# A spectral filter and a gated MLP on one core: the last eight first-stage columns become a fourth fold, and two rounds of w_out are lent to the lone transform pieces

## The chip, the cores and the metric

The kernel runs on one core of a Trainium2 chip. The metric is device time in microseconds of one execution, given as the median of several runs. The engines are TensorE (PE: matrix products, into the eight banks of PSUM), VectorE (DVE), ScalarE (ACT), GpSimd (POOL) and SyncE (SP, which issues transfers). Each takes its instructions in the order in which they were written out; between engines there are semaphores.

## The reference

```python
X = np.fft.rfft(x, axis=1)                 # x: 8 x 3008 x 256, fp32
y = np.fft.irfft(X * (filt_r + 1j*filt_i)[None], n=3008, axis=1)
h = y.reshape(24064, 256) @ w_in           # 256 x 2048
out = (h / (1 + np.exp(-h)) * h) @ w_out   # 2048 x 256
```

So each of 8 batches goes through a Fourier filter along its 3008 tokens, and every token then through a two-layer network with a gate between the layers.

## The kernel before

**The network.** The tokens of a batch form six pairs of blocks (256, 256 and 240 tokens to a block). For one pair the 2048 hidden channels are worked through in eight steps, so a batch has 48 steps and the whole 384. Both layers use a scheme with seven block products instead of eight. `hidden(step)` issues the seven products of w_in, `project(step)` the seven of w_out, one step behind (`LAG`). A step has eight rounds: in each, `hidden` and then `project` advance to their next `yield`, so that the products alternate. The products of w_in are called A11, A12, S2, S1, S3, A22, S4 in the order of their issue; A11, S2, S3 and A22 accumulate in one PSUM bank (`px`, tag x), A12, S1 and S4 in another (`pyz`, tag yz). After each of A11, S2 and S3, ScalarE copies the running sum away (`abc`) before the next product may add to it, and VectorE combines `pyz` with these copies into the operands `g` of the second layer. The products of w_out accumulate over the eight steps in four banks `acc` (tags a0 to a3). Two banks (tag f) are left for the transform.

**The transform.** The length 3008 is 32 x 94. For batches 2 to 7, first-stage products turn the 32 columns of x into residues (into DRAM tensor `d1`), a forward stage takes these (`load_t2`, `forward_two`), the filter is applied, an inverse stage writes `d2`, and a last stage (`load_wide`, `stage3_wide`, `turn_wide`, `copy_wide`, `fold_wide`) writes the network's input `y`. While the network works on one batch, the transform of the next is done in pieces between its steps. Batch b = 0 is done ahead of the steps, and b = 1 by a plan of its own.

**First stage.** Three folds (f = 0, 1, 2) take eight columns each. `load_fold` loads columns and their mirror images (`xr`, a copy of x with reversed rows) into `x_all`; `fold` has four parts on VectorE that form sums and differences; `stage1_fold` has sixteen products of 24 rows by 32 columns, 512 wide, in four banks; `evict_fold` copies two of these to SBUF and `pairs_fold` combines them with the other two and stores, on POOL's queue, to `d1`. The last eight columns go another way: `load_x` and `sums` for u = 6 and 7, `stage1` with four products of 47 rows by 64 columns each (L440, table `wf_t`), and `pairs_t1`.

**What sets the order.** `put(step, round, piece)` enters a piece in a list; `until` plays it out at its time. Steps below are counted within the 48 of the batch whose network is running. A piece is in one of three kinds of place. *Joined* pieces stand at the end of a step (round 7): the last-stage pieces k = 1, 2, 3 at steps 40, 0 and 8, with the folds f = 1 and 2 behind those at 40 and 0. In the next step (*opened*) the first two products of w_out are issued ahead of the first of w_in, and `project` is held in rounds 0 and 2. Pieces placed with `open_step` stand at the start of a step, after two products of w_out: the last eight columns at step 4 and the first last-stage piece, k = 0, at step 38. This last is also *early_out*: two more products of w_out follow the piece, and `project` is held in rounds 0, 2, 3 and 5:

```python
held = work[1:] if rnd in ((0, 2, 3, 5) if step in early_out else (0, 2) if step in opened else ()) else []
```

Which bank a piece uses is given by its `home`: the tags x and yz (`HIDDEN`), an `acc` bank's number, or None for tag f. A bank that the network also uses must be emptied before the next product of `hidden` or `project` can write it: bank a0 of a joined last-stage piece is emptied by VectorE (`turn_wide`), bank a1 by ScalarE (`copy_wide`).

Of the kernel before, what the change touches and what calls it, by code (L numbers as in the profile page):

```python
# [136 lines left out]
def dft_tables():  # L137

    wf = np.zeros((128, 2, 64))
    for par in range(2):  # L140
        for i, idx in enumerate(ORDER):
            ph = 2 * np.pi * (np.arange(N1) * (2 * idx + par) % 94) / 94
            for h in range(2):
                wf[64 * h:64 * h + N1, par, 2 * i] = np.cos(ph)
                wf[64 * h:64 * h + N1, par, 2 * i + 1] = -np.sin(ph)

# [59 lines left out]
    return (wf.astype(f32), wx.reshape(96, 128).astype(f32), wq.astype(f32), wi.astype(f32),  # L206
# [41 lines left out]
def kernel(  # L248
# [12 lines left out]
    wf_host, wx_host, wq_host, wi_host, d_host, e_host = dft_tables()  # L261
    wf_dram = nc.inline_tensor(wf_host, name="wf_tbl")
# [38 lines left out]
    wf_t = cpool.tile([128, 2, 64], FP32)  # L301
# [52 lines left out]
    def spectral(b):  # L354
# [42 lines left out]
        def load_x(u, queue=None):  # L397


            xs[u] = x_t[u % 2]  # L400
            if b == 1:
                xs[u] = xs[u].rearrange("p a n -> p (a n)")
                return load_rows(xs[u], u, 1, queue)
            for h in range(2):
                for r0, nr in ((0, 32), (32, N1 - 32)):
                    nc.sync.dma_start(
                        out=xs[u][64 * h + r0:64 * h + r0 + nr],
                        in_=bass.AP(tensor=x.tensor,
                                    offset=x.offset + (b * S + 32 * r0 + 4 * (u - 3) + 2 * h) * C,
                                    ap=[[32 * C, nr], [32 * N1 * C, 2], [1, 2 * C]]))  # L410
# [7 lines left out]
        def sums(u):  # L418
            ut = x_t[0] if u == 7 else upool.tile([128, 2, 512], FP32, name=f"u_{b}_{u}", tag="u")
            xt = xs.pop(u)  # L420
            for par, op in ((0, ALU.add), (1, ALU.subtract)):
                nc.vector.tensor_tensor(out=ut[0:111, par], in0=xt[0:111, 0], in1=xt[0:111, 1], op=op)
            us[u] = ut

        def stage1(u, ahead=True):
            t1 = tpool.tile([128, 2, 2, C], FP32, name=f"t1_{b}_{u}", tag="t")
            ps = [bank(b, f"pa_{b}_{u}_{h}", HIDDEN[h] if b > 1 and u == 6 else None) for h in range(2)]
            if b == 1:
                xt = xs.pop(u)
                for h in range(2):  # L430
                    nc.tensor.matmul(out=ps[h].rearrange("p n c -> p (n c)"), lhsT=wx_t,
                                     rhs=xt[0:96, 512 * h:512 * h + 512], start=True, stop=True)
                if ahead and u + 2 < 8:
                    load_x(u + 2)
            else:
                ut = us.pop(u)
                for par in range(2):
                    for h in range(2):
                        rows = slice(64 * h, 64 * h + N1)
                        nc.tensor.matmul(out=ps[h][64 * par:64 * par + 64], lhsT=wf_t[rows, par],  # L440
                                         rhs=ut[rows, par], start=True, stop=True)
            if b > 1 and u == 7:
                us["q1"] = t1, ps
                return
            for h in range(2):
                copy = nc.scalar.copy if b == 1 or h == 0 else nc.vector.tensor_copy
                copy(out=t1[:, h], in_=ps[h])  # L447
            if b == 1:
                us["t1", u] = t1
                if ahead:  # L450
                    store_rows(u)
                return
            us["p1"] = t1
# [12 lines left out]

        def pairs_t1(h):
            q, ps = us["q1"]
            p = us["p1"]
            butterfly(p[:, h], q[:, h], ps[1 - h])  # L470
            if h == 0:
                return
            for par in range(2):
                rows = slice(64 * par, 64 * par + 2 * NS)
                nc.gpsimd.dma_start(out=d1[par].rearrange("s p n c -> (s p) n c")[:, 12:16, :],
                                    in_=p[rows].rearrange("p h n c -> p (h n) c"))
                for ri in range(2):
                    nc.gpsimd.dma_start(
                        out=d1[par, :, 1 - ri, 28:32],
                        in_=q[64 * par + ri:64 * par + 2 * NS:2].rearrange("p h n c -> p (h n) c"))  # L480
# [41 lines left out]
        def stage1_fold(f):  # L522
            ut = us.pop("f")
            rhs = x_all[:, 0, 0], x_all[:, 1, 0], ut[:, 0], ut[:, 1]
            home = (*HIDDEN, *ACCS) if f == 0 else (*HIDDEN, 3, None)
            ps = [bank(b, f"pf_{b}_{f}_{q}", home[q]) for q in range(4)]
            for k in range(4):
                for q in range(4):
                    rows = slice(32 * q, 32 * q + 24)
                    nc.tensor.matmul(out=ps[q][32 * k:32 * k + 32], lhsT=wq_t[rows, k], rhs=rhs[k][rows],  # L530
                                     start=True, stop=True)
# [297 lines left out]
        return dict(us=us, store_rows=store_rows, evict_y=evict_y, pairs_t1=pairs_t1, halves=halves, load_first=load_first, stage1_first=stage1_first, fill_first=fill_first, load_x=load_x, load_two=load_two, sums=sums, stage1=stage1, reverse_x=reverse_x,  # L829
# [6 lines left out]
    joined, opened, early_out = set(), set(), set()  # L836
# [8 lines left out]
    def plan(b, part):  # L845
# [109 lines left out]
    def plan_rest(b, part):  # L955
# [6 lines left out]
        else:  # L962
# [7 lines left out]
            for k, step, places in ((1, -8, ((1, 5), (2, 5), (3, 3), (3, 5))), (2, 0, ((1, 5), (3, 5), (5, 3), (5, 5))),  # L970
# [8 lines left out]
                joined.add(at + step)  # L979
                opened.add(at + step + 1)  # L980
# [83 lines left out]
    def project(step):  # L1064
# [368 lines left out]
    for step, t, dram in ((20, wf_t, wf_dram), (20, wq_t, wq_dram), (40, dn_flat, dn_dram),  # L1433
                          (40, en_flat, en_dram), (30, wm_t, wm_dram)):
        put(step, 0, lambda t=t, dram=dram: nc.sync.dma_start(out=t, in_=dram.ap()))
# [19 lines left out]
    combines = ((-2, 1), (6, 1), (11, 5), (22, 5), (26, 6), (38, 1))  # L1455
# [15 lines left out]
    until(-1e-3)  # L1471
    for step in range(n_steps + LAG):
# [7 lines left out]
        if step in opened:  # L1480
# [41 lines left out]
```

## Time and profile before

| | |
|---|---|
| runs | 2527.57, 2528.6, 2530.13 us; median 2528.6 |
| profiled execution | 2527.65 us, of it the span 2525.8 us |
| granted clock of TensorE | 0.997 of full speed over the span |
| PEld, DVE, ACT, POOL busy | 85%, 69%, 43%, 17% of the span |
| transfers | 171.49 MB, mean 68 GB/s |

A group is a line of the kernel with an engine, an operation and its operands. A product of fp32 operands appears as two records. A record's length is the time from its start to its modelled end, longer than the time until the next can start; records that follow each other overlap. In the timeline several records of one group are one line: start, time from the first start to the last end, engine, line, operands, count, and in brackets the idle time of the engine before it with what ended that. Line numbers are those of the kernel before, unless it is said otherwise.

### The profile page before, as it was taken

To read this page: it belongs to the slowest core of one execution; us is meant where nothing else is said; L and a number is where in the kernel's file an instruction comes from. 1 tells how busy PE (TensorE), PEld (TensorE's weight loads), DVE (VectorE), ACT (ScalarE), POOL (GpSimd) and SP (SyncE) were. 2 spreads that over 40 slices of the span, in tenths; PEclk is the share of its full clock that TensorE was granted. 3 is DMA by queue.
4 is the path that set the end of the run, shared out by engine and by line. 5 is a ranking of instruction groups with operands and counts; after the bars stand their busy time and mean duration, and the time that the engine had idled before them with its cause. 6 is when DMAs were issued, how large, how long until landed. Compare 5 with 4: busy or idle time off the path is not lost. (4 is left out here: it accounts for less than half of the span.)

```text
span 2525.8 us, 42128 instructions
## 1 busy us (share of the span) xinstructions
PE 2504.1 (99%) x16122; PEld 2140.9 (85%) x16122; DVE 1750.5 (69%) x3621; ACT 1095.2 (43%) x3012; POOL 433.7 (17%) x679
## 2 busy tenths in 40 slices
PE   8999999999999999999999999999999999999999
PEld 6788888888888888888888888888888888888988
DVE  7866777777767777677777777767677766655544
ACT  3544444444444444444444444444444444444443
POOL 3211211022111121211221112211122111100100
PEclk9999999999999999999999999999999999999999
DMA  9522242212332132420324203331042211200000
GB/s 293 166 68 88 65 107 59 80 51 64 75 86 61 42 80 59 92 74 23 93 55 110 62 25 76 84 75 43 26 103 64 55 43 34 63 21 9 17 9 17
DMA packets 145218, 171.49 MB, mean 68 GB/s; under 512 B 21396, under 2 KB 118772, under 8 KB 144132
## 3 DMA queue, kind: packets, MB, share of 16 engines
q1 hardware_dynamic: 119752, 117.85, 18.0%
q0 software_dynamic: 22272, 45.68, 7.1%
q10 hardware_dynamic: 2992, 5.28, 0.7%
q8 instruction: 126, 2.06, 0.3%
q14 instruction: 76, 0.62, 0.1%
HBM read 96.88 MB, written 81.26 MB: 71 GB/s over the span
## 5 line engine op out<-in xcount | busy, mean ns | idle before, releaser
L1083 PE MATMUL acc<-g,w_t 128*128 128x256 f32 (+1 forms) x5376 | 1509.0, 376 | 4.2 <-DVE q L818 3.7
L1083 PEld LDWEIGHTS acc<-g,w_t 128*128 128x128 f32 x5376 | 1017.0, 190 | 150.4 <-DVE q L818 18.9
L989 DVE TENSOR_TENSOR g<-pyz,abc 128x256 f32<-128x256 f32 (+1 forms) x1152 | 479.1, 416 | 501.1 <-ACT abc L1039 259.8
L989 DVE TENSOR_TENSOR g<-g 128x256 f32<-128x256 f32 (+3 forms) x1152 | 589.6, 512 | 196.6 <-ACT g L1022 183.4
L1018 PE MATMUL px<-ty,w_t 128*128 128x256 f32 (+1 forms) x2304 | 679.2, 376 | 1.7 <-ACT abc L1033 0.7
L1022 ACT ACTIVATE g<-g 128x256 f32<-128x256 f32 (+1 forms) x1152 | 472.9, 410 | 243.1 <-DVE g L989 243.1
L989 POOL TENSOR_TENSOR s<-s 128x256 f32<-128x256 f32 (+1 forms) x329 | 251.7, 782 | 1467.0 <-DVE s L1101 1099.9
L1018 PEld LDWEIGHTS px<-ty,w_t 128*128 128x128 f32 x2304 | 432.8, 190 | 65.5 <-ACT abc L1033 7.0
L1018 PE MATMUL pyz<-y,w_t 128*128 128x256 f32 (+1 forms) x1536 | 452.7, 376 | 0.8 <-DVE g L989 0.6
L1018 PEld LDWEIGHTS pyz<-y,w_t 128*128 128x128 f32 x1536 | 283.2, 189 | 46.2 <-DVE g L989 6.9
L1033 ACT COPY abc<-px 128x256 f32<-128x256 f32 (+1 forms) x384 | 141.1, 368 | 368.1 <-PE px L1018 368.1
L1039 ACT COPY abc<-px 128x256 f32<-128x256 f32 (+1 forms) x384 | 141.5, 368 | 313.2 <-PE px L1018 313.1
L1022 ACT ACTIVATE g<-px 128x256 f32<-128x256 f32 (+1 forms) x384 | 145.8, 380 | 302.3 <-PE px L1018 302.3
L1018 PE MATMUL px<-y,w_t 128*128 128x256 f32 (+1 forms) x768 | 227.4, 378 | 1.5 <-DVE y L775 1.5
L1018 PE MATMUL pyz<-ty,w_t 128*128 128x256 f32 (+1 forms) x768 | 226.0, 376 | 0.2 <-DVE g L989 0.2
L1018 PEld LDWEIGHTS px<-y,w_t 128*128 128x128 f32 x768 | 143.9, 190 | 26.7 <-ACT t L447 4.9
L1018 PEld LDWEIGHTS pyz<-ty,w_t 128*128 128x128 f32 x768 | 142.2, 190 | 21.4 <-DVE g L989 1.0
L1026 ACT COPY abc<-px 128x256 f32<-128x256 f32 (+1 forms) x384 | 135.1, 352 | 37.3 <-PE px L1018 37.3
L1101 ACT COPY s<-acc 128x512 f32<-128x512 f32 (+1 forms) x94 | 54.2, 577 | 47.6 <-issue 28.6
L646 POOL DMA_DIRECT2D d<-low x36 | 22.2, 618 | 289.0 <-DVE low L642 289.0
L818 DVE STREAM_TRANSPOSE q<-pd 128x512 f32<-128x512 f32 x84 | 57.1, 699 | 3.2 <-PE pd L797 3.2
L827 DVE TENSOR_TENSOR y<-q 128x384 f32<-128x384 f32 x112 | 56.1, 542 | 0.0
(159 smaller groups left out, 1367.8 us busy)
## 6 DMA issues: line engine op xcount, KB each, us to landing
t<-d SPq DMA_DIRECT2D x84, 256.0 KB
t<-d SPq DMA_DIRECT2D x224, 96.0 KB
out_dram<-s SPq DMA_DIRECT2D x64, 256.0 KB
d<-q POOLq DMA_DIRECT2D x48, 256.0 KB, 5.2
d<-low POOLq DMA_DIRECT2D x36, 256.0 KB, 4.2
xr<-in_x_dram SPq DMA_DIRECT2D x6, 1472.0 KB
out_dram<-s SPq DMA_DIRECT2D x30, 240.0 KB
x_all<-in_x_dram SPq DMA_DIRECT2D x72, 96.0 KB
```

Source lines behind the costliest of these rows:

```text
L646: nc.gpsimd.dma_start(out=d2[a0:a0 + 8, 16 * end:16 * end + 16], in_=part)
L818: nc.vector.transpose(out=t.rearrange("p (n a c) -> p n a c", n=8, a=2), in_=us["pd", k][r].rearrange("p a c -> p (a c)").rearrange("p (n ...
L827: nc.vector.tensor_tensor(out=dst[:, :, :, at:at + n], in0=even[:, :, :, 0:n], in1=odd[:, :, :, 0:n], op=op)
L989: eng.tensor_tensor(out=out, in0=in0, in1=in1, op=op)
L1018: nc.tensor.matmul(out=out, lhsT=w_t[:, jp, c, 0], rhs=rhs, start=start, stop=True, skip_group_check=True)
L1022: nc.scalar.activation(out=g[:, k, 0:n], in_=g[:, k, 0:n] if src is None else src, func=AFT.Silu)
L1026: nc.scalar.copy(out=sums[:, 0, 0:n], in_=xo)
L1033: nc.scalar.copy(out=sums[:, 1, 0:n], in_=xo)
L1039: nc.scalar.copy(out=sums[:, 2, 0:n], in_=xo)
L1083: nc.tensor.matmul(out=acc[pair][i][:, h, 0:n], lhsT=w_t[:, jp, c, 1], rhs=g[:, k, 0:n], start=(jp == 0 and h == 0), stop=last, skip_group ...
L1101: copy(out=s[:, 2 * i:2 * i + 2, 0:n], in_=acc[pair][i][:, :, 0:n])
```

## The change

The last eight columns of batches 2 to 7 become a fourth fold, f = 3. It has a step of its own, step 5 of the running batch, and its parts on VectorE are in steps 3 and 4. `load_x` for these batches, `sums`, `pairs_t1` and the table `wf_t` go. Of its two copies out of PSUM one is ScalarE's and one VectorE's.

Step 5 and step 38 are now both *early_out*, in another sense: in the step before (4 and 37, called the lending step here) `project` is held in rounds 3, 6 and 7, so that two products of w_out are left over. These are issued at the start of the early_out step, ahead of the piece. Two products of the current `project` follow the piece, and then rounds 0 and 2 are held.

In the step after a joined last-stage piece (k = 1, 2, 3) the first two products of w_out change places, so that bank a1 is written before a0.

Some pieces move: one transpose of k = 2 from step 3 to step 2, its two `fold_wide` from step 5 to steps 6 and 7; the loads of `t2` from step 6, round 0, to step 7, round 3; the load of the fold f = 0 for batches 3 to 7 from step 6 to step 7, round 4, behind these; and the token sums of the fourth pair from round 5 to round 1 of step 22.

```diff
-            home = (*HIDDEN, *ACCS) if f == 0 else (*HIDDEN, 3, None)
+            home = {0: (*HIDDEN, *ACCS), 3: (*HIDDEN, None, None)}.get(f, (*HIDDEN, 3, None))
...
-                nc.scalar.copy(out=us["p"][:, q], in_=us["ps"][q])
+                copy = nc.vector.tensor_copy if f == 3 and q == 1 else nc.scalar.copy
+                copy(out=us["p"][:, q], in_=us["ps"][q])
...
-            early_fold = (-73, ((-68, 3), (-68, 5), (-67, 5), (-66, 5))), (-90, ((-82, 5), (-81, 3), (-81, 5), (-75, 5)))
+            early_fold = (-73, ((-68, 3), (-68, 5), (-67, 5), (-66, 5))), (-89, ((-82, 5), (-81, 3), (-81, 5), (-75, 5)))
...
-                put(at + load, 0, part["load_fold"], f)
+                put(at + load, 4 if load == -89 else 0, part["load_fold"], f)
...
-            for u, step, rnd in ((6, -46, 5), (7, -45, 3)):
-                put(at - 47, 0, part["load_x"], u)
-                put(at + step, rnd, part["sums"], u)
-            open_step(at - 44, (part["stage1"], 6), (part["stage1"], 7))
-            put(at - 44, 3, part["pairs_t1"], 0)
-            put(at - 44, 5, part["pairs_t1"], 1)
+            put(at - 47, 0, part["load_fold"], 3)
+            for k, (step, rnd) in enumerate(((-45, 3), (-45, 5), (-44, 3), (-44, 5))):
+                put(at + step, rnd, part["fold"], 3, k)
+            early_out.add(at - 43)
+            open_step(at - 43, (part["stage1_fold"], 3), (part["evict_fold"], 3))
+            put(at - 43, 3, part["pairs_fold"], 3, 0)
+            put(at - 43, 5, part["pairs_fold"], 3, 1)
...
-        put(at - 42, 0, part["load_t2"], 0)
-        put(at - 42, 0, part["load_t2"], 1)
+        put(at - 41, 3, part["load_t2"], 0)
+        put(at - 41, 3, part["load_t2"], 1)
...
-            for k, step, places in ((1, -8, ((1, 5), (2, 5), (3, 3), (3, 5))), (2, 0, ((1, 5), (3, 5), (5, 3), (5, 5))),
+            for k, step, places in ((1, -8, ((1, 5), (2, 5), (3, 3), (3, 5))), (2, 0, ((1, 5), (2, 5), (6, 5), (7, 3))),
...
+                turned.add(at + step)
...
             order = PROJECT[0:2] + PROJECT[3:5] + PROJECT[2:3] + PROJECT[5:]
+            if step in turned:
+                order = order[1::-1] + order[2:]
...
-    combines = ((-2, 1), (6, 1), (11, 5), (22, 5), (26, 6), (38, 1))
+    combines = ((-2, 1), (6, 1), (11, 5), (22, 1), (26, 6), (38, 1))
...
-        if step in opened:
+        if step in early_out:
+            for _ in left.pop():
+                pass
+        elif step in opened:
             for _ in range(2):
                 next(work[1])
...
+        keeps = step + 1 in early_out
         for rnd in range(ROUNDS):
-            held = work[1:] if rnd in ((0, 2, 3, 5) if step in early_out else (0, 2) if step in opened else ()) else []
+            held = work[1:] if rnd in ((3, 6, 7) if keeps else (0, 2) if step in opened else ()) else []
             work = [w for w in work if w in held or next(w, work) is not work]
             until(step + rnd / ROUNDS)
+        if keeps:
+            left.append(work.pop())
```

More of the change, by code (lines that the diff above doesn't have):

```diff
@@ L137, in dft_tables @@
 def dft_tables():
[L139 to L145, printed above, removed]
     wx = np.zeros((96, 4, 32))
@@ L205, in dft_tables @@
     f32 = np.float32
-    return (wf.astype(f32), wx.reshape(96, 128).astype(f32), wq.astype(f32), wi.astype(f32),
+    return (wx.reshape(96, 128).astype(f32), wq.astype(f32), wi.astype(f32),
             d.reshape(128, NS, 2, 32).astype(f32),
@@ L259 @@
     ctx.enter_context(tc.manual_schedule())
-    wf_host, wx_host, wq_host, wi_host, d_host, e_host = dft_tables()
-    wf_dram = nc.inline_tensor(wf_host, name="wf_tbl")
+    wx_host, wq_host, wi_host, d_host, e_host = dft_tables()
     wx_dram = nc.inline_tensor(wx_host, name="wx_tbl")
@@ L299 @@
     accps = pool("accps", 1, PSUM)
-    wf_t = cpool.tile([128, 2, 64], FP32)
     wx_t = cpool.tile([96, 128], FP32)
@@ L397, in load_x @@
         def load_x(u, queue=None):
[L400 to L410, printed above, removed]
+            xs[u] = x_t[u % 2].rearrange("p a n -> p (a n)")
+            load_rows(xs[u], u, 1, queue)
         def load_two():
@@ L416, in load_two @@
                 xs[u] = x_t[u].rearrange("p a n -> p (a n)")
[L418 to L423, printed above, removed]
         def stage1(u, ahead=True):
             t1 = tpool.tile([128, 2, 2, C], FP32, name=f"t1_{b}_{u}", tag="t")
[L427 to L444, printed above, removed]
-            for h in range(2):
[L446 to L453, printed above, removed]
+            ps = [bank(b, f"pa_{b}_{u}_{h}") for h in range(2)]
+            xt = xs.pop(u)
+            for h in range(2):
+                nc.tensor.matmul(out=ps[h].rearrange("p n c -> p (n c)"), lhsT=wx_t,
+                                 rhs=xt[0:96, 512 * h:512 * h + 512], start=True, stop=True)
+            if ahead and u + 2 < 8:
+                load_x(u + 2)
+            for h in range(2):
+                nc.scalar.copy(out=t1[:, h], in_=ps[h])
+            us["t1", u] = t1
+            if ahead:
+                store_rows(u)
         def store_rows(u):
@@ L465, in butterfly @@
             nc.vector.tensor_tensor(out=p, in0=p, in1=back, op=ALU.add)
[L467 to L480, printed above, removed]
         def reverse_x():
@@ L834 @@
     pending = []
-    joined, opened, early_out = set(), set(), set()
+    joined, opened, early_out, turned = set(), set(), set(), set()
     ACCS, HIDDEN = (2, 3), ("x", "yz")
@@ L1432 @@
         put(7, 0, part["load_t4"], g)
-    for step, t, dram in ((20, wf_t, wf_dram), (20, wq_t, wq_dram), (40, dn_flat, dn_dram),
+    for step, t, dram in ((20, wq_t, wq_dram), (40, dn_flat, dn_dram),
                           (40, en_flat, en_dram), (30, wm_t, wm_dram)):
@@ L1471 @@
     until(-1e-3)
+    left = []
     for step in range(n_steps + LAG):
```

2 lines of the change are left out of this document (1 added, 1 removed).

## The prediction

> **What bounds the kernel now.** I read the page's busy shares first, then its costliest groups, then the order in time of TensorE (PE), stretch by stretch.
>
> ```profile
> PE 2504.1 (99%) x16122; PEld 2140.9 (85%) x16122; DVE 1750.5 (69%) x3621; ACT 1095.2 (43%) x3012; POOL 433.7 (17%) x679
> ...
> L1083 PE MATMUL acc<-g,w_t 128*128 128x256 f32 (+1 forms) x5376 | 1509.0, 376 | 4.2 <-DVE q L818 3.7
> ```
>
> PE is the bound. But its ends are modelled, so "99%" hides short stops; they show only where start follows start too slowly. In undisturbed stretches one w_in or w_out product (two records) starts 0.43 us after the one before, and a step of fourteen takes 6.04 us. I therefore price every piece of the transform by what it adds to that beat. The present last-eight-columns piece, at step 4 of a batch (PE in order of time; columns are start, length, instruction):
>
> ```profile
> 1036.38 1.03 PE L1083 MATMUL acc<-g,w_t 128*128 128x256 f32 x4
> 1037.34 1.09 PE L440 MATMUL pa<-u,wf_t 47*64 47x512 f32 x8
> 1038.25 1.04 PE L440 MATMUL pa<-x_all,wf_t 47*64 47x512 f32 x8
> 1039.22 0.70 PE L1018 MATMUL px<-y,w_t 128*128 128x256 f32 x2
> 1039.75 0.59 PE L1018 MATMUL pyz<-y,w_t 128*128 128x256 f32 x2
> ```
>
> Four acc records should last 0.86, so pa could start at 1037.24: 0.10 is lost entering. pa to px is 1.88, and px takes 0.53 instead of 0.43, a restart of 0.10. Together 2.08 us. The first last-stage piece (step 38):
>
> ```profile
> 1252.44 1.03 PE L1083 MATMUL acc<-g,w_t 128*128 128x256 f32 x4
> 1253.40 1.14 PE L797 MATMUL pd<-t,wm_t 24*32 24x512 f32 x32
> 1254.47 1.13 PE L1083 MATMUL acc<-g,w_t 128*128 128x256 f32 x4
> 1255.47 0.70 PE L1018 MATMUL px<-y,w_t 128*128 128x256 f32 x2
> ...
> 1256.88 0.59 PE L1018 MATMUL px<-ty,w_t 128*128 128x256 f32 x2
> 1257.31 0.59 PE L1018 MATMUL pyz<-ty,w_t 128*128 128x256 f32 x2
> 1257.93 0.70 PE L1018 MATMUL px<-ty,w_t 128*128 128x256 f32 x2
> 1258.47 0.59 PE L1083 MATMUL acc<-g,w_t 128*128 128x256 f32 x2
> 1259.09 0.70 PE L1018 MATMUL px<-ty,w_t 128*128 128x256 f32 x2
> ```
>
> The piece itself costs 0.09 entering, 1.07 to the next acc, 0.10 restart, then 0.14 because px waits for its bank. But two more stops follow: px at 1257.93 and at 1259.09 each start 0.62 after the product before them (0.19 late) and take 0.10 to restart, since with rounds 3 and 5 held only one product stands between S2 and S3, and between S3 and A22, and ScalarE's copy of the sum needs longer. That is 0.59 us lost to order alone.
>
> A last-stage piece in the last batch, with no first-stage piece behind it (PE, then ScalarE, then VectorE), and one with it:
>
> ```profile
> 2234.62 1.14 PE L797 MATMUL pd<-t,wm_t 24*32 24x512 f32 x32
> 2237.00 1.13 PE L1083 MATMUL acc<-g,w_t 128*128 128x256 f32 x4 [1.25 <-DVE q L818]
> 2235.96 0.58 ACT L810 COPY o<-pd 128x512 f32<-128x512 f32 x1 [0.37 <-PE pd L797]
> 2236.24 1.30 DVE L818 STREAM_TRANSPOSE q<-pd 128x512 f32<-128x512 f32 x2
> ```
>
> ```profile
> 1015.76 1.14 PE L797 MATMUL pd<-t,wm_t 24*32 24x512 f32 x32
> 1016.64 0.90 PE L530 MATMUL pf<-x_all,wq_t 24*32 24x512 f32 x8
> ...
> 1018.15 1.13 PE L1083 MATMUL acc<-g,w_t 128*128 128x256 f32 x4
> ```
>
> Alone, acc waits for VectorE's transpose of bank a0, although ScalarE has emptied a1 by 2236.55.
>
> **The change part by part.**
>
> *A fold instead of two column pieces, six batches (2 to 7).* Out go eight pa products; in come sixteen pf products (24 rows by 32 columns, 512 wide) in step 5. No row shows pf straight after ordinary work. Its twin in shape is pd at 1253.40: the same 32 records of 24x512 on 24*32, 1.07 us to the next acc. The other bound is pf behind pd, 1016.64 to 1018.15, 1.51. I take the pd row, since shape and predecessor agree: 0.10 + 1.07 + 0.10 = 1.27. The two acc products of the new step follow pf directly; meanwhile ScalarE and VectorE empty the x and yz banks (0.59 and 0.69 by the copies of the same kind, L537 and L447). px starts about 2.0 us after pf's first start, both copies are done near 1.9, and yz is wanted 0.43 later still, so I add nothing there.
>
> One edge remains. In the lending step 4, VectorE does the fold's third part in round 3 and its fourth in round 5. Such a pair takes 1.28:
>
> ```profile
> 1249.24 1.28 DVE L520 TENSOR_TENSOR uf<-x_all 120x512 f32<-120x512 f32 x2
> 1250.89 0.42 DVE L989 TENSOR_TENSOR g<-pyz,abc 128x256 f32<-128x256 f32 x1 [0.36 <-ACT abc L1039]
> ```
>
> Counted from the lending step's first start, the first pair runs 2.84 to 4.1, the middle combine to 4.55, the second pair to 5.8, and the combine that frees yz to about 6.1 to 6.2. pf wants yz at 6.14. I add 0.10 for this: 1.37 in place of 2.08, **6 x 0.71 = 4.2 us** saved. Ends: nothing added 4.9 saved; pace of the joined pf and a wait of 0.2, 1.90, 1.0 saved.
>
> *Rounds lent to both pieces.* Rounds 3 and 6 of w_out are now skipped one step earlier and its last two products run right before the piece; the piece's own step holds only rounds 0 and 2. So S2 to S3 and S3 to A22 again have two products between them, as in step 4 of before, whose order this is and which shows no such stop. The 0.59 goes in seven batches: **7 x 0.59 = 4.2 us**. What it may bring is a wait in the lending step, where S2, acc, S1, S3, acc, acc, A22, S4 follow each other: S3 comes 1.29 after S2, and the row at 1257.93 shows that 1.05 is enough. S4 comes 1.73 after S3; the copy and combine need 1.46 to 1.53 after S3 (combine starts 1.04 after it and takes 0.42), or 0.07 later when VectorE is in the pair above. So no wait, by about 0.1 after the restart's lead. Ends: no wait, 4.2; two waits of 0.29 in each lending step, nothing left.
>
> *Bank order.* With a1 first, acc in the three lone pieces of the last batch can start when ScalarE ends (2236.55) and not VectorE (2236.95); by the three sites 0.34, 0.40 and 0.42, **1.2 us**. With pf behind pd, acc starts 0.52 after pf's last record (a drain like the 0.52 after pd and pa), so nothing there. Ends: 0 and 1.2.
>
> *What costs nothing.* VectorE: four sums of 0.68 become six operations, 1.23, 1.22 and four of 0.68, 2.4 us more per batch; it is 69% busy and each round 3 and 5 has a gap, freed by moving one transpose to step 2 and two y folds to steps 6 and 7. The moved token sums (step 22, round 1) fit as those at (6, 1) do. SyncE: eight loads of 96 KB for eight of the same bytes; one table less. POOL: eight stores of about 0.50 us for six, and a step later. Then the loads of t2 (four, about 0.6 us apart) are issued in step 7 and the next batch's eight x loads behind them. Stores were landed by 1051.3; one step (6.04) and two stores (1.0) later is 1058.4. Four issues and a landing, from 1050.93 to about 1057 before, end near 1064. The forward piece that reads t2 starts at 1069.65: 5 us of cover. The x loads have until seven steps later.
>
> Sum: 4.2 + 4.2 + 1.2 = 9.6 us. The profiled execution took 2527.65 (span 2525.8 and 1.85 around it), so 2518.1. It lies 0.95 under the median of the three runs, 2528.6, from which I take the same: **2519.0**. About 0.2%, 5.1 us, is what a measurement can tell from no change (three runs spread over 2.6).
>
> **The rivals.**
>
> *pf keeps the pace it has when joined* (1.51, not 1.07). For: no row shows it alone. Against: inverse and forward pieces too are slow only behind other packed work. Costs 6 x 0.44 = 2.6: 2521.6.
>
> *The lent rounds make new waits.* VectorE is full in step 4, and 0.1 is little. One wait of 0.29 in each of the 13 lending steps costs 3.8: 2522.8, two cost 7.5: 2526.5, where nothing could be told.
>
> *Slower: t2 comes too late.* The chain from fold to stores to loads to the forward piece loses its step of slack in all six batches. Beyond 5 us of lateness each further us costs 6. It eats the gain at 5 + 9.6/6 = 6.6 us and makes the kernel slower by 0.2% at 7.5, 2533.7; at 8 it gives 2537. Against: the stores and loads above would need twice their time.
>
> *Products in the same row group do not overlap.* Then the sixteen pf products go in four waves of two passes, each like pa's (0.43 to 0.48 apart): 0.48 + 6 x 0.43 + 0.54 = 3.6, with entry and restart 3.8; 6 x 1.72 worse than pa, and with the other two parts 2533.5, on the edge of slower. Against: pd reuses its row groups four times and its 32 records take 1.14. In a sentence of its own: this is what the Trainium skill states (TensorE: Matmul & The Clock Gate, Part 3, "What overlaps and what doesn't": a weight load overlaps matmuls under way only when its row group differs); by that rule 2533.5, by the pd row 2519.0, and the trace disagrees with the rule.
>
> **How the numbers follow.** Forecast 0.70; joined pace 0.10; new waits 0.11 (one per step 0.05, two 0.06); t2 late 0.04; row groups 0.02; some slower thing unnamed 0.03. The range runs from 2517, the gain with nothing added and 1.3 of scatter, to 2524.5, which takes in the joined pace or single waits with 1.5 of scatter. Faster: 0.70 + 0.10 + 0.05 = 0.85; within 0.2%: two waits and half of the row groups, 0.07; slower 0.08.
>
> **What the changed profile would show.** Right: pf alone with 32 records and acc 1.07 after its start; px after step 38's S1 without a stop; acc in the last batch waiting for ACT, about 0.4 earlier; steps of 6.04 around. Wrong: a wait of pf or S4 for VectorE in step 4, pf at 1.5, or the forward piece waiting for a DMA.

## The result, and the profile after

| | before | after |
|---|---|---|
| median, us | 2529.09 (2527.08 to 2532.26) | 2520.72 (2518.05 to 2522.60) |
| profiled execution, us | 2527.65 | 2518.08 |
| its span, us | 2525.8 | 2516.0 |

The ratio of the two is 0.9965, with an interval from 0.9953 to 0.9977: faster by 0.35%. The forecast was 2519.0 and its sum for the profiled execution 2518.1. That the second number is met to 0.02 us is luck, as the accounting below shows: the steps that the change touches gave 8.92 of the 9.6 us, by terms that were off in both directions, and an opening that happened to be 0.94 us shorter in this execution gave nearly all the rest.

The page of the changed kernel, busy shares and the w_out group:

```profile
PE 2494.1 (99%) x16218; PEld 2139.7 (85%) x16218; DVE 1764.1 (70%) x3633; ACT 1096.8 (44%) x3012; POOL 440.7 (18%) x691
...
L1030 PE MATMUL acc<-g,w_t 128*128 128x256 f32 (+1 forms) x5376 | 1507.4, 376 | 3.0 <-ACT o L753 2.5
```

TensorE still bounds it. The releaser of the longest idle before acc is no longer VectorE's transpose but ScalarE's copy (L753): the turned bank order.

The new fold, in the same batch as the column piece shown before; timeline, all engines (start, length, engine, line, operands, idle before with its releaser; here and below weight loads are left out):

```profile
1037.52 1.28 DVE L462 TENSOR_TENSOR uf<-x_all 120x512 f32<-120x512 f32 x2
...
1038.30 1.03 PE L1030 MATMUL acc<-g,w_t 128*128 128x256 f32 x4
...
1038.72 0.42 DVE L934 TENSOR_TENSOR g<-pyz,abc 128x256 f32<-128x256 f32 x1
...
1039.26 0.69 PE L472 MATMUL pf<-x_all,wq_t 24*32 24x512 f32 x8
...
1039.80 0.64 PE L472 MATMUL pf<-uf,wq_t 24*32 24x512 f32 x8
1040.37 1.13 PE L1030 MATMUL acc<-g,w_t 128*128 128x256 f32 x4
1040.74 0.59 ACT L480 COPY tf<-pf 128x512 f32<-128x512 f32 x1 [1.15 <-PE pf L472]
...
1041.38 0.70 PE L963 MATMUL px<-y,w_t 128*128 128x256 f32 x2
```

From pf's first start to acc it takes 1.11 us. The edge in the lending step is none: VectorE's second pair ends at 1038.80 and the combine that frees yz at 1039.14, 0.12 us ahead of pf. But px starts 1.02 after acc, where two acc products, four records with one restart, need 0.97; it then takes 0.54 and not 0.43 to the next product, a restart of 0.10. It waited for ScalarE, whose copy of bank x starts only 1.48 us after pf's first start.

The first last-stage piece, in another batch than before, TensorE in order of time:

```profile
640.97 1.14 PE L740 MATMUL pd<-t,wm_t 24*32 24x512 f32 x32
642.04 1.13 PE L1030 MATMUL acc<-g,w_t 128*128 128x256 f32 x4
643.04 0.70 PE L963 MATMUL px<-y,w_t 128*128 128x256 f32 x2
...
645.74 0.59 PE L963 MATMUL px<-ty,w_t 128*128 128x256 f32 x2
646.17 1.03 PE L1030 MATMUL acc<-g,w_t 128*128 128x256 f32 x4
647.03 0.59 PE L963 MATMUL px<-ty,w_t 128*128 128x256 f32 x2
```

After the px at 643.04 every start follows the last by 0.43 a product: the two stops of before are gone. The one at 643.04 itself (wait 0.04, restart 0.10) is still there.

A lone last-stage piece in the last batch, the one shown before:

```profile
2225.70 1.14 PE L740 MATMUL pd<-t,wm_t 24*32 24x512 f32 x32
...
2227.05 0.59 ACT L753 COPY o<-pd 128x512 f32<-128x512 f32 x1 [0.36 <-PE pd L740]
2227.32 1.31 DVE L761 STREAM_TRANSPOSE q<-pd 128x512 f32<-128x512 f32 x2
...
2227.68 1.13 PE L1030 MATMUL acc<-g,w_t 128*128 128x256 f32 x4 [0.84 <-ACT o L753]
```

From pd to acc 1.98 us, 2.38 before.

**Accounting.** I take the start of the first w_in product of each of the 384 steps and subtract the two traces step by step. Up to the start of step 2 both kernels do the same, but for the load of the table `wf_t`. The time of that opening changes from execution to execution (90.95 us before, 90.01 after, up to 96.10 in the kernels below). From there to the end it is 2434.89 before and 2425.97 after, **8.92 us less**; ordinary steps agree to 0.001 us. The other 0.65 of the 9.57 between the profiled executions is the opening (0.94) less 0.3 outside the spans.

| steps | forecast, us | measured, us |
|---|---|---|
| 3 to 5, six batches (fold) | -4.2 | -3.86, and +0.34 in one batch |
| 37 and 38, seven batches (lent rounds) | -4.2 | -4.17 |
| behind the three lone pieces (bank order) | -1.2 | -0.34 - 0.40 - 0.43 = -1.17 |
| 23, eight batches (token sums) | 0 | -1.26 |
| 22, first batch (token sums) | 0 | +0.75 |
| the rest | 0 | +0.33 in step 169, +0.11 in all others |

The terms add up to the 8.92 within rounding. So three things had to be explained: what holds back px behind the fold, what the token sums do, and what the two steps 101 and 169 lost.

### The profile page after: what moved, and what is told of

Its sections match the earlier page's. It is cut to its first block, busy times and chain, and to the rows that moved or that the text cites. A ratio compares the mean times of both kernels' runs of the same rounds, so it can differ in the third digit from the quotient of the medians.

```text
span 2516.0 us, 42348 instructions
## 1 busy us (share of the span) xinstructions
PE 2494.1 (99%) x16218; PEld 2139.7 (85%) x16218; DVE 1764.1 (70%) x3633; ACT 1096.8 (44%) x3012; POOL 440.7 (18%) x691
## 3 DMA queue, kind: packets, MB, share of 16 engines
q8 instruction: 127, 2.08, 0.3%
## 4 chain that ended last, share of the span: by engine, by line
PE 96%; DVE 2%; DMA 2%; ACT 0%; issue 0%; SPq 0%; POOL 0%; DVEq 0%; ACTq 0%
PE acc L1030 45%; PE px L963 26%; PE pyz L963 19%; PE pd L740 1%; PE pf L472 1%; PE pc L568 1%; PE pb L530 1%; PE pc L646 0%; DMA w_t<-in_x_dram 0%; DMA filt<-in_filt_i_dram 0%; PE pb L512 0%; DVE g L934 0%; PE pa L402 0%; DMA d_t<-d_tbl 0%; DVE w_t L1201 0%
## 5 line engine op out<-in xcount | busy, mean ns | idle before, releaser
L492 POOL DMA_DIRECT2D d<-tf x96 | 48.8, 509 | 216.0 <-DVE tf L422 195.2
L462 DVE TENSOR_TENSOR uf<-x_all 120x512 f32<-120x512 f32 (+1 forms) x72 | 60.2, 864 | 0.3 <-issue 0.3
```

Source lines behind the costliest of these rows:

```text
L462: nc.vector.tensor_tensor(out=out, in0=in0, in1=in1, op=op)
L492: nc.gpsimd.dma_start(out=d1[par, :, grp, at:at + 4], in_=part[rows].rearrange("p q n c -> p (q n) c"))
```

## The experiments

Times below are lengths of steps (start to start, us) in the profile of each kernel, or the time from the start of step 2 to the end, so that the opening is left out.

**One part alone: the lending for step 38.** Kernel before, with

```diff
-        if step in opened:
+        if step in early_out:
+            for _ in left.pop():
+                pass
+        elif step in opened:
...
+        keeps = step + 1 in early_out
...
-            held = work[1:] if rnd in ((0, 2, 3, 5) if step in early_out else (0, 2) if step in opened else ()) else []
+            held = work[1:] if rnd in ((3, 6, 7) if keeps else (0, 2) if step in opened else ()) else []
...
+        if keeps:
+            left.append(work.pop())
```

> The kernel before with one part of the change: the lending of rounds 3 and 6 for the first last-stage piece (step 38); the last eight columns stay as they were, and so do the bank order and the token sums. Prediction (the rounds held in step 38 made px wait twice for ScalarE's copies, 0.595 us in all, and the lending makes no wait of its own in step 37): steps 37 and 38 together go from 9.078 + 5.016 to 8.212 + 5.284 us, 0.60 a batch, 7 x 0.595 = 4.2 us. Rival (new waits in the lending step): 0.29 less for each of them, 2.1 us or nothing gained. Nothing changes in steps 3 to 5 and 23.

Steps 37 and 38 went from 9.075 + 5.016 to 8.212 + 5.284 in each of the seven batches, 0.595 a batch, 4.17 in all; from step 2 to the end 4.11 less than before. The term stands, and the lending makes no new wait in step 37.

**One part alone: the bank order.** Kernel before, with

```diff
+                turned.add(at + step)
...
+            if step in turned:
+                order = order[1::-1] + order[2:]
```

> The kernel before with one part of the change: the first two products of w_out change places in the steps behind a joined last-stage piece. Prediction: in the three lone pieces of the last batch acc then waits for ScalarE's copy and no longer for VectorE's transpose, 0.34, 0.40 and 0.42 us earlier, 1.2 us in all; in the other batches, where pf stands behind pd or nothing waits, within 0.02 us of nothing. Rival (the turned order only moves the wait to the second of the two products): nothing gained.

Three steps changed, by -0.338, -0.400 and -0.427, and no other from step 3 on by more than 0.012. From step 2 to the end 1.22 less. The term stands.

**One part alone: the token sums.** Kernel before, with

```diff
-    combines = ((-2, 1), (6, 1), (11, 5), (22, 5), (26, 6), (38, 1))
+    combines = ((-2, 1), (6, 1), (11, 5), (22, 1), (26, 6), (38, 1))
```

> The kernel before with one part of the change: the token sums of the fourth pair in round 1 of step 22 instead of round 5. The prediction priced this at nothing. The traces of both kernels have step 23 at 5.828 us before and 5.670 after. Theory A (the sums in round 5 made VectorE's last combine of step 22 late, and pyz waited 0.05 us for it and took 0.09 to restart): step 23 is 5.670 in every batch, 8 x 0.157 = 1.26 us gained, and no other step moves. Rival B (step 23 is shorter for another part of the change): step 23 stays at 5.828 and nothing is gained.

Theory A held for step 23: 5.670 in all eight batches, 1.26 gained. But the first batch's step 22 grew from 5.670 to 6.413, which neither theory had. VectorE there, before (timeline, from 2.7 us into step 22, which starts at 232.19):

```profile
234.92 0.69 DVE L662 TENSOR_TENSOR z<-pb,filt 128x512 f32<-128x512 f32 x1
235.53 0.68 DVE L662 TENSOR_TENSOR p<-pb,filt 128x512 f32<-128x512 f32 x1
236.43 0.41 DVE L989 TENSOR_TENSOR g<-pyz,abc 128x240 f32<-128x240 f32 x1 [0.23 <-ACT abc L1039]
236.75 0.68 DVE L989 TENSOR_TENSOR ty<-y 128x512 f32<-128x512 f32 x1
237.47 0.88 DVE L989 TENSOR_TENSOR ty<-y,ty 128x256 f32<-128x256 f32 x2
238.27 0.40 DVE L989 TENSOR_TENSOR g<-pyz,abc 128x240 f32<-128x240 f32 x1
```

The sums (ty) run across the start of step 23 at 237.86; the combine behind them comes 0.2 us late, and so pyz in step 23. With the sums in round 1 (VectorE, then TensorE; step 22 starts at 234.00):

```profile
236.73 0.69 DVE L989 TENSOR_TENSOR ty<-y 128x512 f32<-128x512 f32 x1
237.45 0.89 DVE L989 TENSOR_TENSOR ty<-y,ty 128x256 f32<-128x256 f32 x2
238.25 0.68 DVE L662 TENSOR_TENSOR z<-pb,filt 128x512 f32<-128x512 f32 x1
238.85 0.68 DVE L662 TENSOR_TENSOR p<-pb,filt 128x512 f32<-128x512 f32 x1
239.45 0.40 DVE L989 TENSOR_TENSOR g<-pyz,abc 128x240 f32<-128x240 f32 x1
...
239.91 0.67 PE L1018 MATMUL pyz<-y,w_t 128*128 128x240 f32 x2 [0.48 <-DVE g L989]
```

In the first batch alone two filter products of the next transform stand in round 3 of this step. With the sums ahead of them the combine starts 5.45 us into the step instead of 4.24, and pyz waits 0.64 and restarts in 0.09. So the move gives 1.26 and takes 0.74: 0.52 net, 0.53 by the time from step 2 to the end.

**The fold without the lending.** Changed kernel, with

```diff
-            early_out.add(at - 43)
```

> The changed kernel with the rounds of w_out not lent to the new fold step: step 5 is merely opened, pf still has its step to itself, but stands behind two products of w_out of its own step and px comes directly behind pf. It tells how much of the fold's gain of 0.62 us a batch (2.08 to 1.46 us beyond two ordinary steps) is due to the step of its own and how much to the lending. Theory A (the gain is the lending: px can't start before ScalarE has emptied bank x about 2.07 us after pf's first start, and the two acc products fill that time): steps 4 to 6 grow by 0.60 to 0.75 us a batch, 3.6 to 4.5 us in all, and the fold's gain is gone. Rival B (pf by itself is the gain, being shorter than the two pa pieces): 0 to 0.2 us a batch, at most 1.2 us.

Steps 4 to 6 together grew by 0.86 us in five batches and 0.81 in the last, 5.1 us in all, more than the 3.6 to 4.5 of theory A. TensorE and ScalarE there:

```profile
1042.47 0.66 PE L472 MATMUL pf<-x_all,wq_t 24*32 24x512 f32 x8
...
1043.95 0.58 ACT L480 COPY tf<-pf 128x512 f32<-128x512 f32 x1 [1.37 <-PE pf L472]
...
1044.59 0.70 PE L962 MATMUL px<-y,w_t 128*128 128x256 f32 x2 [0.98 <-ACT tf L480]
```

Without two acc products behind pf, px stands idle until bank x is empty. Beyond two ordinary steps this fold costs 2.32 us, against 2.08 for the column piece of before and 1.46 in the changed kernel. So the step of its own by itself is a loss of 0.24; the whole gain, and more, is in the lending, which puts two products behind pf that cover ScalarE's copy.

**The order of pf's products.** Changed kernel, the fold f = 3 with

```diff
-            for k in range(4):
-                for q in range(4):
+            for i in range(16):
+                k, q = divmod(i, 4) if f < 3 else divmod(i, 4)[::-1]
```

> The changed kernel with the sixteen pf products of the fold f = 3 in another order: four products in a row share their row group and their bank, instead of one in four. In the changed kernel the 32 records start about 7 ns apart and pf takes 1.11 us to the next acc. Theory A (products of the same row group overlap as well as others if they write different columns): pf stays at 1.11 us, steps 4 and 5 within 0.05 us of 8.260 and 5.284; bank x is complete earlier, so px may lose its small wait, at most 0.15 us a batch. Rival B (products of the same row group stand in line, and the order of the changed kernel hid it): four in a row take at least 0.43 us each time after the first, 16 products 3 us or more, six times 2 us = 12 us slower.

Step 4 takes 8.280 (8.260 in the changed kernel), step 5 5.180 (5.284): rival B, 12 us slower, falls. TensorE, from the first of the 32 records:

```profile
1045.11 0.62 PE L472 MATMUL pf<-x_all,wq_t 24*32 24x512 f32 x2
1045.12 0.62 PE L472 MATMUL pf<-uf,wq_t 24*32 24x512 f32 x2
1045.14 0.62 PE L472 MATMUL pf<-x_all,wq_t 24*32 24x512 f32 x2
1045.15 0.62 PE L472 MATMUL pf<-uf,wq_t 24*32 24x512 f32 x2
...
1046.29 1.13 PE L1030 MATMUL acc<-g,w_t 128*128 128x256 f32 x4
1047.26 0.59 PE L963 MATMUL px<-y,w_t 128*128 128x256 f32 x2
```

A product has two records, and they come in two groups of sixteen, each product once in either; within a group the records mostly start 7 ns apart, and 0.25 to 0.31 us lie between the groups in either order of the products. The first four records here are the four products of one row group, the next four those of another, and all eight start within 0.05 us. pf takes 1.18 instead of 1.11. And px has no wait: bank x is complete after the first four products here, and ScalarE's copy starts 1.20 us after pf's first start. It is the second half of the result that mattered: px's wait depends on when PE tells ScalarE that x is complete.

**What holds back the copy.** A raise of a semaphore is how an engine tells those that wait that an instruction is done. In the changed kernel PE raises its semaphore eleven times during pf where a load of the next fold follows, as the records of semaphores show: once at 0.084 us after pf's first start, eight times from 1.055 to 1.353, 42.5 ns apart, at 1.462 for ScalarE's copy and at 1.504 for VectorE's. Each of the eight x_all loads waits on the pf product that last read its place. In the last batch, with no such load, there are two raises, for the two copies; ScalarE's starts at 1.28, and px does not wait. The experiment takes away what the loads wait for, with another tile for what pf reads:

```diff
+                us["v"] = tpool.tile([128, 2, 512], FP32, name=f"vf_{b}_{f}", tag="t") if f == 3 else x_all[:, :, 0]
...
-                    ((xt[:, 0, 0], ut[:, 0], ut[:, 1], ALU.add),
-                     (xt[:, 1, 0], ut[:, 0], ut[:, 1], ALU.subtract)),
+                    ((vt[:, 0], ut[:, 0], ut[:, 1], ALU.add),
+                     (vt[:, 1], ut[:, 0], ut[:, 1], ALU.subtract)),
...
-            rhs = x_all[:, 0, 0], x_all[:, 1, 0], ut[:, 0], ut[:, 1]
+            rhs = vt[:, 0], vt[:, 1], ut[:, 0], ut[:, 1]
```

> The changed kernel with one edit: the third part of the fold f = 3 writes its two results to a tile of its own and no longer back into x_all, so that pf reads nothing from x_all and the eight loads of the next fold wait for VectorE instead of for eight single pf products. In the changed kernel PE raises its semaphore 11 times during pf where a load of x_all follows (steps 53, 101, 149, 197, 245), the raises appear 42.5 ns apart, and ScalarE's copy of bank x starts 1.48 us after pf's first start; in the last batch, where no load follows, it starts 1.28 us after. Theory A (the row of raises holds back the copy, the copy holds back px): copy starts near 1.28 in all six batches, px follows the two acc products without a stop, and steps 4 and 5 together go from 8.260 + 5.284 to 8.211 + 5.180 us in five batches, 5 x 0.152 = 0.76 us in all; the profiled span of 2516.0 becomes 2515.2 where nothing else scatters. Rival B (the copy is late because of what ScalarE or the bank does, or because the last batch differs in another way): the steps stay at 8.260 and 5.284 and nothing is gained. Rival C: the tile is shared with the stores of the fold before; if these are not done, the fold's third part waits and pf starts late, more than 8.30 for step 4.

```profile
1042.70 0.66 PE L474 MATMUL pf<-vf,wq_t 24*32 24x512 f32 x8
...
1043.78 1.13 PE L1032 MATMUL acc<-g,w_t 128*128 128x256 f32 x4
1044.01 0.58 ACT L482 COPY tf<-pf 128x512 f32<-128x512 f32 x1 [0.97 <-PE pf L474]
...
1044.74 0.60 PE L965 MATMUL px<-y,w_t 128*128 128x256 f32 x2
```

Three raises instead of eleven; the copy starts 1.30 us after pf's first start, px follows acc by 0.97 and takes 0.44. Steps 4 and 5 are 8.175 + 5.188 in all six batches, 0.18 less in five of them, 0.03 in the last: 0.93 us, a little above the 0.76 expected, because pf itself is also shorter (1.07 to acc, not 1.11). Theory A stands, B falls, and pf does not start late, as C would have it. Beyond two ordinary steps the fold now costs 1.28, where the pd row of before had promised 1.27 without any extra.

The Trainium skill (TensorE: Matmul & The Clock Gate, "The cost: per-tile semaphore tail") says that increments of a semaphore from many tiles are carried out one after the other, at 26.3 ns each. The trace agrees that they stand in line; here it is 42.5 ns each.

**Which engine empties bank x in step 38.** Changed kernel, with

```diff
-            open_step(at - 10, (part["stage3_wide"], 0, (*HIDDEN, None, None)), (part["turn_wide"], 0, 0),
-                      (part["copy_wide"], 0, 1))
-            for step, rnd, piece, *args in ((-10, 5, "turn_wide", 2), (-9, 3, "turn_wide", 3, 1),
+            open_step(at - 10, (part["stage3_wide"], 0, (*HIDDEN, None, None)), (part["copy_wide"], 0, 0),
+                      (part["turn_wide"], 0, 1))
+            for step, rnd, piece, *args in ((-10, 5, "turn_wide", 2), (-9, 3, "turn_wide", 3, 0),
```

> The changed kernel with one edit: in the first last-stage piece (step 38) bank x is emptied by ScalarE's copy and bank yz by VectorE's transpose, instead of the other way round. In the changed kernel px waits 0.036 to 0.038 us for bank x there and takes 0.104 to restart, steps 37 and 38 are 8.212 and 5.284. VectorE's transpose runs from 7.44 to 8.16 of step 37, ScalarE's copy from 7.48 to 8.07. Theory A (px waits for VectorE's transpose and for nothing else): px has no stop, steps 37 and 38 become 8.175 and 5.180, 7 x 0.14 = 1.0 us gained. Rival B (only the name of the later engine changes, because pyz then waits for its bank, wanted 0.43 us after px's): nothing gained, or up to 0.1 us lost in each of the seven.

```profile
1249.20 1.14 PE L740 MATMUL pd<-t,wm_t 24*32 24x512 f32 x32
...
1250.27 1.13 PE L1030 MATMUL acc<-g,w_t 128*128 128x256 f32 x4
...
1250.51 0.59 ACT L753 COPY o<-pd 128x512 f32<-128x512 f32 x1 [1.18 <-PE pd L740]
1250.55 0.72 DVE L761 STREAM_TRANSPOSE q<-pd 128x512 f32<-128x512 f32 x1 [0.50 <-PE pd L740]
1251.24 0.60 PE L963 MATMUL px<-y,w_t 128*128 128x256 f32 x2
1251.68 0.59 PE L963 MATMUL pyz<-y,w_t 128*128 128x256 f32 x2
```

px's start is 0.44 ahead of pyz, no restart; the copy is done at 1251.10, the transpose at 1251.27, ahead of pyz's 1251.68. Steps 37 and 38 are 8.175 + 5.188, 0.13 less in each of seven batches, 0.93 us against 1.0 expected. Rival B falls.

**Both edits together.**

> The two edits before this one together in one kernel. If both small waits are what the theories A say, they are in different steps and add up: 0.76 + 1.0 = 1.8 us less than the changed kernel in the profile (span 2516.0 to 2514.2 where nothing else scatters), and 0.9965 of the kernel before becomes about 0.9958. If one of the rivals holds, 0.8 to 1.0 us, which the timed runs can't tell from nothing; the steps' lengths can.

The median is 2519.12 us, the ratio to the kernel before 0.9956 (0.9942 to 0.9970). From step 2 to the end it is 2423.89, 2.08 less than the changed kernel; 1.87 of it are the two edits' own steps; of the rest, the 0.34 of step 101 is gone, a stop of 0.25 in step 272 is new (ScalarE starts a copy late there, see the late starts below), and 0.1 is scatter in step 2.

**The first batch's sums elsewhere.** Both edits, and

```diff
-        step, rnd = combines[pair % per] if pair != 1 else (7, 5)
+        step, rnd = combines[pair % per] if pair not in (1, 3) else ((7, 5), (21, 4))[pair // 3]
```

> The kernel with the fold's own tile and the turned emptying of step 38, and one more edit: for the first batch alone the token sums of the fourth pair stand in step 21, round 4, and not in step 22, round 1. The runs so far show the moved sums to gain 0.157 in step 23 of every batch and to cost 0.745 in step 22 of the first batch, where two filter products of the next batch (z and p from pb, 0.68 each) come behind them on VectorE and push the combine that pyz waits for from 4.64 to 5.85 of the step. Theory A (it is that order and nothing else; VectorE is idle from 3.48 to 5.46 of step 21, and the sums take 1.5): step 22 of the first batch goes from 6.415 to 5.670, steps 21 and 23 stay, 0.75 us gained; from the start of step 2 to the end 2.2 to 2.6 us less than the changed kernel, and the ratio to the kernel before about 0.9955. Rival B (the sums hold up step 21 instead, since the combine at 5.46 follows them): step 21 grows by as much as step 22 loses.

It missed: step 22 became 7.022 instead of 5.670. From step 2 to the end the kernel takes 1.69 less than the changed kernel and not 2.2 to 2.6, and its median is 2518.37, the ratio to the kernel before 0.9957 (0.9943 to 0.9970). The idle stretch of VectorE in step 21 lies ahead of a combine that stands before round 4 in the order written out; the sums queued behind it and ran from 5.78 to 7.4 us. The gap in the timeline was real, but the order written out did not reach it. With (19, 1) in place of (21, 4):

> As the kernel before it, but the sums of the fourth pair of the first batch in round 1 of step 19. In step 21, round 4, they were written behind the combine at 5.46 and so ended at 6.9 and later, and pushed the filter products into step 22, which grew to 7.022. In step 19 VectorE has nothing from 2.83 to 4.24, the sums take 2.73 to 4.34 in round 1 of the steps where they fit, and y is complete by 215.8 us, before that step. Theory A (VectorE's order in step 22 is all that costs): step 22 is 5.670 and steps 19, 21 and 23 stay at 5.670, 6.892 and 5.670, 0.75 us less than with round 1 of step 22; from the start of step 2 to the end 2423.1 (2423.9 before this edit, 2426.0 for the changed kernel, 2434.9 for the kernel before). Rival B (these sums cost wherever they stand in the first batch): the steps around grow by as much, 2423.9 or more.

Step 22 is 5.670, and steps 19, 21 and 23 stay. From step 2 to the end 2423.25 us: 0.64 less than both edits, 2.72 less than the changed kernel, 11.64 less than the kernel before. The median is 2517.34, the ratio to the kernel before 0.9952 (0.9938 to 0.9965). This is the best of the kernels; against the changed kernel it was not timed side by side, and 0.1% would hardly show there.

**The late starts.** In the changed kernel VectorE's first combine of step 101 (timeline):

```profile
737.99 0.59 PE L963 MATMUL pyz<-y,w_t 128*128 128x256 f32 x2
...
739.04 0.42 DVE L934 TENSOR_TENSOR g<-pyz,abc 128x256 f32<-128x256 f32 x1 [1.49 <-PE acc L1030]
```

It starts 1.05 after pyz, and in other batches 0.70; pyz's next product waits for it, and the step is 5.626 instead of 5.284. Step 169 is the same. The experiment shifts VectorE's stream of instructions:

```diff
+    blank = cpool.tile([128, 1], FP32)
+    for i in range(32):
+        pending.append((57 + i // 4 + (4 + i % 4 / 8) / ROUNDS, 999, lambda: nc.vector.memset(blank, 0.0)))
```

> The changed kernel with 32 small extra instructions on VectorE (each sets 128 x 1 elements that nobody reads, about 0.06 us or less) in rounds 4 of steps 57 to 64, where VectorE has idle time. In the changed kernel VectorE's first combine starts 0.34 late in step 101 and 0.33 late in step 169, in no other batch, and at the same two steps in the profiles of all kernels whose VectorE works off the same instructions. Theory A (the late start belongs to a place in VectorE's stream of instructions): with 32 more ahead, both steps fall back to 5.284 and 5.180, and a late start of up to 0.35 turns up elsewhere or is hidden. Rival B (it belongs to what other engines or transfers do at that time): steps 101 and 169 stay at 5.626 and 5.509. All other steps from 66 on stay within 0.02 us.

```profile
744.36 0.59 PE L963 MATMUL pyz<-y,w_t 128*128 128x256 f32 x2
...
745.07 0.42 DVE L934 TENSOR_TENSOR g<-pyz,abc 128x256 f32<-128x256 f32 x1 [1.14 <-PE pyz L963]
```

Both late starts are gone (5.284 and 5.180), and no other appears from step 66 on. The small instructions themselves cost 1.1 us in steps 59 to 65: each is 0.06 long but they start 0.13 apart. Theory A stands as far as it goes: the late start belongs to a place in the program.

The other runs say which place. Counted by its records, waits included, the late combine is VectorE's number 1344 in step 101 and number 2112 in step 169, 3 x 256 records further on. VectorE's wait just before the first ends 1.19 us into the step, as in the batches before and behind it, so that wait does not make it late. In the kernel with the fold's own tile, and in the three kernels that build on it, two more waits stand ahead of the first combine, which is then punctual, while the second is still number 2112 and late. ScalarE does the same: its copies number 2112 in step 240 of the kernel with the fold's own tile and number 2368 in step 272 of the three others start 0.28 late, and these steps are 0.27 and 0.25 longer. With the 32 small instructions, VectorE's number 2368 (step 188) starts 0.35 late, where it costs nothing. All these places are multiples of 256 records apart. At most such places no late start is seen, and that it is the fetching of instructions is argued, not shown: transfers of the instruction queues lie near (736 to 740 us for step 101), but they lie near many steps.

## Why the prediction was right, and where it was not

*The fold.* The step "I take the pd row" was right: pf alone has pd's pace, entry 0.09, 1.07 to 1.11 to acc, restart 0.10. The step "I add 0.10 for this" (pf waiting for yz in the lending step) was wrong: pf does not wait, the combine ends 0.12 us before it. And "both copies are done near 1.9 ..., so I add nothing there" was wrong in five of the six batches: ScalarE's copy ends 2.07 after pf's first start, since its release stands in line behind eight raises for x_all loads, and px waits 0.05 and restarts in 0.10. In the last batch, without these loads, the copy ends at 1.87 and px does not wait, as forecast. So 0.62 a batch came out (0.77 in the last) for 0.71. The loads had been priced at SyncE, as "eight loads of 96 KB for eight of the same bytes"; their price was on TensorE, in what they wait for.

*The lent rounds* were right in mechanism and size (0.595 a batch, no wait in the lending step), for step 38. For step 5 the prediction counted on the two products behind pf to cover the copies, but gave them no price of their own. They are the fold's whole gain: without the lending 5.1 us are lost.

*The bank order* was right at all three sites.

*The token sums* are the term that was missed: "fit as those at (6, 1) do" was true of seven batches, where it even gained 0.157 because the old place had been late, and false in the first, where it costs 0.74. Both were to be read from the trace of before: step 23 at 5.828 beside 5.670 for its neighbours, and VectorE's rows in step 22 of the first batch.

*The rivals.* The joined pace (1.51) is out by the 1.11 measured. New waits in the lending steps: none. t2 late: SyncE issued the four t2 loads from 1054.16 to 1056.74, and pb's first product starts at 1065.8 with no idle time of TensorE before it that a transfer ended. Row groups in line: out by the order of the products above. There the Trainium skill (TensorE: Matmul & The Clock Gate, Part 3, "What overlaps and what doesn't") lets a weight load overlap matmuls under way only in another row group; four records of one row group that start within 0.03 us, each 0.61 us long, are against it.

*The median.* The medians differ by 8.37 us, for 8.92 from step 2 on and an opening that scatters. In the stretch from 75 to 95 us the granted clock is 1.00 in the profile of the changed kernel and lower in all others, down to 0.67:

```profile
75.00:95.00 20.00, 17.11 (x65) 11.86 (x66) 18.47 (x46) 9.93 (x25) 6.05 (x12) 1.00 0.90 277
```

```profile
75.00:95.00 20.00, 18.12 (x171) 13.29 (x165) 14.57 (x35) 9.12 (x22) 5.21 (x12) 0.67 0.73 214
```

The columns behind the engines' busy times are the clock, the share of the DMA engines and GB/s; the second row is the kernel with the 32 small instructions, whose opening took 95.41 us. The profiled execution of the changed kernel had the shortest opening of all, which is why the sum seemed met to the last digit while the median lies 1.7 above the forecast.

## What to carry to other kernels

Here eight transfers far off the critical path waited for products of TensorE, and the raise that mattered stood in line behind theirs: let pieces that must be freed fast read tiles that only a computing engine refills. A piece between dense products is paid by what covers the emptying of its banks, so put two independent products behind it before anything else. Price a moved item in every batch where it lands, the odd first one too, by the order written out on its engine, and read the step lengths of before for the place where it stands now.

## What the runs showed of the hardware that I had not expected

- Raises of TensorE's semaphore are 42.5 ns apart, eight of them 0.3 us, and delayed another engine by 0.18 us.
- A late start of 0.28 to 0.35 us on an engine can belong to a place in the program: VectorE's records number 1344 and 2112 (steps 101 and 169), the first gone with two more waits ahead, both gone with 32 more instructions ahead, and ScalarE's number 2112 and 2368 in the kernels with the fold's own tile. In the profiles of the kernel before and of its three variants step 114 is 0.08 to 0.09 longer than its like in other batches; that this has the same cause is not shown.
- VectorE instructions of 0.06 us on 128 x 1 elements start 0.13 us apart.
- The first 90 us scatter by up to 6 us between executions, with a granted clock from 0.67 to 1.00 between 75 and 95 us, and from step 3 on a step that no edit touches repeats to 0.02 us, but for the late starts and the last step (up to 0.12). So a comparison from there on can tell about 0.5 us with one profile each, where the intervals of the medians' ratios are some 3 us to either side.
